# Seven-product matmul on one Trainium2 core: a new order of the products, T4 in its own bank, each operand sum in its own step, squares six steps ahead

## Chip, cores, metric

One core of a Trainium2 chip runs the whole program. The metric is device microseconds (us) of one execution, as a median of several. The kernel before takes 1394.89 us: three runs between 1392.15 and 1395.37.

## What is computed

```
attn = attention(q, k, v, phi)                    # linear attention over 32 memory slots, 8 x 8 heads, 576 tokens
x    = attn as 4608 tokens x 512
h    = x @ w_in1;   g  = max(h, 0)**2             # 512 -> 2048
x2   = g @ w_out1                                 # 2048 -> 512   "first out product"
h2   = x2 @ w_in2;  g2 = h2 * sigmoid(h2)         # 512 -> 2048
out  = g2 @ w_out2                                # 2048 -> 512   "second out product"
```

All in float32.

## The kernel before, in words

Five stretches follow each other in time: attention and `x @ w_in1` (to about 323 us of the span), the first out product (324 to about 683 us), `x2 @ w_in2` (683 to about 1042 us), the second out product (from about 1027 us to the end, its first steps interleaved with the last of the stretch before). The two out products are one function, `second()`, called with `square=True` for the first (its input is relu only, the square is still to be taken) and with `square=False` for the second.

**Seven products for eight.** `second()` cuts the tokens into 6 batches. In each batch input and weight are cut into 2 x 2 blocks, and four blocks of result C11, C12, C21, C22 come from seven block products instead of eight. The seven left operands are B11, B21, B22 and four sums: T1 = B12 - B11, T2 = B22 - T1, T3 = B22 - B12, T4 = B21 - T2. The right operands are combinations of the weight blocks, made in the background and held in six slots per weight tile (a seventh, product 6, is loaded into slot 1 when product 1 is done, by `next_w`). Product numbers are those of `PRODUCTS`: 0 B11, 1 B21, 2 T2, 3 T1, 4 T3, 5 B22, 6 T4, and before the change this is also the order in which they run.

**Steps.** Each product has four steps h; a step is 12 matmuls of 128x128 by 128x384 on TensorE (two weight tiles, two output halves, three each), so that a product has 48 matmuls and a batch 336. Float32 accuracy comes from splitting an operand into a high and a low part: the operand tile `c` of a step holds both. ScalarE casts the raw tile `r` to the high part (line L822), then VectorE subtracts to get the low part (L823). Of each group of three matmuls the second needs the low part. `AHEAD = 4`: in program order the operand of a step is made four steps before its matmuls. `c` tiles rotate through six buffers (`spool`), and these six are also those in which `x2 @ w_in2` keeps its results (`g2t`).

**Sums.** The raw tiles are 128x768. VectorE makes T1 at L810, T2 at L814, T3 at L816, T4 at L819, in place except T2, which has tiles of its own. In program order T1 and T2 are both made in the step of product T2, T3 in the step of T1, T4 in the step of T3. In the first out product ScalarE squares every raw tile in place (L796): in program order B11 and B21 in the steps of B11, B12 and B22 in the steps of B21.

**Accumulation.** The products gather in PSUM banks a, b, c (`psa`, `psb`, `psc`): B11, T2, T3, T4 in a, B21 in b, T1 and B22 in c. `evict` takes partial sums out between: u1 is a copy of a after B11, and C11 = u1 + b; u2 is a copy of a after T2, and C12 = u2 + c after B22; u3 is a copy of c after T1, and C22 = u3 + a after T3; C21 is a itself after T4, copied by ScalarE into `y` (L872) and stored by SyncE (L874). Copies are ScalarE's (L734, L739, L741), additions VectorE's (L732).

**What sets the order.** The text gives program order, waits and buffers; a scheduler, which plans with estimated times, then picks the final order of instructions on each engine. On an engine they run strictly in that order. In the background, during the first out product, ScalarE and VectorE also build the weights of the next stretch (L162 to L216).

Of the kernel before, what the change touches and what calls it, by code (L numbers as in the profile page):

```python
# [77 lines left out]
def attention_moe_moe(ctx: ExitStack, tc, q, kv, phi, w_in1, w_out1, w_in2, w_out2, out):  # L78
# [645 lines left out]

    PRODUCTS = (("B11", "a"), ("B21", "b"), ("T2", "a"), ("T1", "c"), ("T3", "a"), ("B22", "c"), ("T4", "a"))
    FIRST = (0, 1, 3)
    UTAG = {"u1": "u1", "u2": "u2", "u3": "u1"}

    def evict(n, t, s, c, copy3, done):


        add = lambda to, x, y: nc.vector.tensor_tensor(to, x, y, op=ALU.add)  # L732
        if n == 0:
            nc.scalar.copy(s("u1"), t["a"])  # L734
        elif n == 1:
            add(c("C11"), t["b"], s("u1"))
            done("C11", None)
        elif n == 2:
            nc.scalar.copy(s("u2"), t["a"])  # L739
        elif n == 3:  # L740
            copy3(s("u3"), t["c"])  # L741
        elif n == 4:
            add(c("C22"), t["a"], s("u3"))
            done("C22", None)
        elif n == 5:
            add(c("C12"), t["c"], s("u2"))
            done("C12", None)
        else:
            done("C21", t["a"])

    QS = 2
    NH = NQ // QS
# [10 lines left out]
    def second(src, order, square, to, weights, begin, tiles=tuple(range(10))):  # L763
# [27 lines left out]
                        if held:  # L791
                            held(dma)

        def squares(b, h, names):
            for name in names if square else ():
                ins = nc.scalar.activation(raw[b, name, h], raw[b, name, h], AF.Square)  # L796
                if b == 0 and name in SQUARED:
                    follow(ins, relus[SQUARED[name] + h])

        def combos(b, n, h):  # L800

            tt = nc.vector.tensor_tensor
# [32 lines left out]
        begin(quarters)  # L835
        for k in range(AHEAD):
            ahead(k)
        for k, (b, n, h) in enumerate(steps):
            ahead(k + AHEAD)
            bank = PRODUCTS[n][1]  # L840
            if h == 0 and n == 0:
                ps = [{} for _ in range(2)]
                st = [{} for _ in range(2)]
            if h == 0 and n in FIRST:
                for o in range(2):
                    ps[o][bank] = psum.tile([P, TH], F32, tag=bank, bufs=4 if bank == "a" else 2, name=f"ps{bank}")
            x = cc.pop((b, n, h))
            for u in range(QS):
                for o in range(2):
                    for m, (wi, xi) in enumerate(((0, 0), (0, 1), (1, 0))):  # L850
                        mm = nc.tensor.matmul(  # L851
                            ps[o][bank], W[h * QS + u][:, slot(n), wi, o * P:(o + 1) * P], x[:, xi, u],
                            start=(n in FIRST and h == u == m == 0), stop=(h == NH - 1 and u == QS - 1 and m == 2),
                            skip_group_check=True,
                        )
                        if u == o == m == 0:
                            begun.append(mm)
            next_w(weights, range(h * QS, h * QS + QS), n, b == TB - 1)
            if h < NH - 1:
                continue  # L860
            for o in range(2):
                def tile_s(u, o=o):
                    if u not in st[o]:
                        st[o][u] = upool.tile([P, TH], F32, tag=UTAG[u], name=u)
                    return st[o][u]

                def done(c, bank, o=o, b=b):
                    if bank is None:
                        y = tile_s(SUM[c], o)
                    else:  # L870
                        y = upool.tile([P, TH], F32, tag="u1", name="y")
                        nc.scalar.copy(y, bank)  # L872
                    oh, half = int(c[1]) - 1, int(c[2]) - 1
                    nc.sync.dma_start(to(b, 2 * oh + o, half), y)  # L874
                evict(n, ps[o], tile_s, lambda c: tile_s(SUM[c]), nc.scalar.copy, done)
# [7 lines left out]
    def begin_out1(quarters):  # L883
# [9 lines left out]
        for q in range(WR, WR + 2):  # L893
            for k in range(SLOTS):
                held(load_w(w1o, q, k))
        for k, name in enumerate(("B11", "B21", None)):
            for q in (*range(WR + 2, NQ), *range(WR)) if k == 1 else range(WR + 2, NQ):
                held(load_w(w1o, q, k))
            if name:
                quarters(0, (name,), held)  # L900
            if k == 1:
                quarters(0, ("B12", "B22"), held)
        for k in range(3, SLOTS):
            for q in range(WR + 2, NQ):
                held(load_w(w1o, q, k))

# [50 lines left out]
    for b in range(TB):  # L957
        for r in range(NQ // 2):
# [4 lines left out]
            for n, (_, bank) in enumerate(PRODUCTS):  # L963
# [12 lines left out]
                for q in qs:  # L976
                    def tile_s(u, q=q):
                        if u not in st[q]:
                            st[q][u] = upool.tile([P, TH], F32, tag=UTAG[u], name=u)
                        return st[q][u]  # L980

                    def done(c, src, q=q):
# [19 lines left out]

    def begin_out2(quarters):
        quarters(0, ("B11", "B21"))
        for q0, n0, n1 in ((0, 0, 4), (2, 0, 4), (4, 0, 2), (6, 0, 1), (6, 1, 2), (4, 2, 4), (6, 2, 3)):
# [5 lines left out]
        for n in range(3, SLOTS):  # L1011
            for q in (range(NQ) if n > 3 else (6, 7)):
                load_w(w2o, q, n)

    second(g2, tuple(c.replace("C", "B") for c in order2), False,
# [46 lines left out]
```

## Time and profile before

| what | value |
|---|---|
| median of 3 runs (lowest, highest) | 1394.89 us (1392.15, 1395.37) |
| the profiled execution: its own time | 1397.46 us |
| its span, first to last instruction | 1395.6 us |
| mean granted TensorE clock | 0.994 of full speed |
| TensorE (PE) busy | 1365.2 us, 98% of the span, 9349 matmuls |
| VectorE (DVE) busy | 967.8 us, 69% |
| ScalarE (ACT) busy | 791.9 us, 57% |
| DMA | 388 MB, mean 278 GB/s |

The profiled execution is 2.57 us above the median, and 1.86 us of it lie outside its span. PE is the engine that is nearly always busy; the other two have room on average, which says nothing yet about a single place.

### The profile page before, as it was taken

Reading aid. Unit: us, or ns where it says so; the run is one execution under the profiler, and the core shown is the slowest. Engines: PE = TensorE matmul, PEld = TensorE weight load, DVE = VectorE, ACT = ScalarE, POOL = GpSimd, SP = SyncE. Lnnn points to the kernel's source line nnn. Section 1 sums busy time; section 2 is a strip of 40 time slices with the busy share of each in tenths; the row PEclk is TensorE's granted clock in tenths of the full one; section 3 lists DMA queues with packets and bytes.
Section 4 is the critical chain, followed back from the end, with each engine's and each line's share of the span. In section 5 each row is a group of like instructions: output and inputs, shape, how many; then the busy total and the mean of one; then the engine's idle time right before and its main releaser. Section 6 shows DMA issues by size and latency. Waiting matters only on the chain.

```text
span 1395.6 us, 25373 instructions
## 1 busy us (share of the span) xinstructions
PE 1365.2 (98%) x9349; PEld 1317.2 (94%) x9349; DVE 967.8 (69%) x1578; ACT 791.9 (57%) x1305; POOL 21.8 (2%) x44
## 2 busy tenths in 40 slices
PE   7899999998999999999999999999998999999998
PEld 5778888898999999999999999999998999999998
DVE  4668777746698897979565756566447858768583
ACT  3656666667758768586355545555444444444442
POOL 0001000000000000000000000000000000000000
PEclk9999999999999999999999999999999999999999
DMA  9979999899888869789988787888998567564640
GB/s 318 367 235 335 351 351 323 299 340 338 268 276 286 285 229 337 259 291 319 354 298 298 257 305 269 281 290 281 365 398 311 160 227 235 190 230 155 227 155 35
DMA packets 208445, 388.25 MB, mean 278 GB/s; under 512 B 19264, under 2 KB 90944, under 8 KB 208320
## 3 DMA queue, kind: packets, MB, share of 16 engines
q1 hardware_dynamic: 208320, 386.62, 80.3%
q8 instruction: 74, 1.21, 0.3%
q14 instruction: 51, 0.42, 0.1%
HBM read 253.38 MB, written 133.17 MB: 277 GB/s over the span
## 4 chain that ended last, share of the span: by engine, by line
PE 83%; DMA 11%; DVE 3%; ACT 1%; issue 1%; SPq 0%; ACTq 0%; DVEq 0%
PE psa L851 28%; PE psc L851 14%; PE psa L970 14%; PE h L661 7%; PE psc L970 7%; PE psb L851 6%; PE psb L970 4%; DMA g<-gt 3%; DMA r<-g 2%; DMA kv<-kv 2%; DMA st<-moe_w_in 2%; PE pswp L463 1%; DMA a<-phi 1%; DMA ws<-w1o 1%; PE pskv L407 1%
## 5 line engine op out<-in xcount | busy, mean ns | idle before, releaser
L823 DVE TENSOR_TENSOR c<-r,c 128x768 fp32r<-128x768 f32 x336 | 316.2, 953 | 164.2 <-ACT c L822 162.4
L851 PE MATMUL psa<-c,ws 128*128 128x384 f32 x2304 | 416.5, 338 | 6.7 <-DVE c L823 4.4
L851 PEld LDWEIGHTS psa<-c,ws 128*128 128x128 f32 x2304 | 406.6, 190 | 8.2 <-DVE c L823 5.4
L822 ACT CAST c<-r 128x768 fp32r<-128x768 f32 x336 | 278.3, 835 | 221.4 <-PE psa L851 112.1
L970 PE MATMUL psa<-xc,ws 128*128 128x384 f32 x1152 | 217.3, 336 | 0.0
L661 PEld LDWEIGHTS h<-at,wp 128*128 128x128 f32 x1344 | 180.2, 188 | 31.0 <-ACT gt L671 18.2
L851 PE MATMUL psc<-c,ws 128*128 128x384 f32 x1152 | 205.7, 335 | 1.8 <-ACT c L822 1.8
L851 PEld LDWEIGHTS psc<-c,ws 128*128 128x128 f32 x1152 | 200.9, 188 | 2.2 <-ACT c L822 2.2
L970 PEld LDWEIGHTS psa<-xc,ws 128*128 128x128 f32 x1152 | 202.3, 188 | 0.0
L661 PE MATMUL h<-at,wp 128*128 128x288 f32 x1344 | 191.2, 299 | 6.4 <-ACT gt L671 6.4
L970 PE MATMUL psc<-xc,ws 128*128 128x384 f32 x576 | 110.9, 335 | 0.0
L851 PE MATMUL psb<-c,ws 128*128 128x384 f32 x576 | 105.3, 337 | 0.0
L851 PEld LDWEIGHTS psb<-c,ws 128*128 128x128 f32 x576 | 101.6, 189 | 0.0
L970 PEld LDWEIGHTS psc<-xc,ws 128*128 128x128 f32 x576 | 101.2, 188 | 0.0
L796 ACT ACTIVATE r<-r 128x768 f32<-128x768 f32 x96 | 79.4, 844 | 22.9 <-DMA r<-g 18.9
L671 ACT ACTIVATE gt<-h 128x576 f32<-128x576 f32 x112 | 72.2, 648 | 35.0 <-PE h L661 24.4
L205 DVE TENSOR_TENSOR pp<-pw,pp 128x256 f32<-128x256 f32 x148 | 62.9, 434 | 32.7 <-ACT pp L204 30.3
L204 ACT CAST pp<-pw 128x256 fp32r<-128x256 f32 x148 | 58.3, 405 | 39.4 <-PE psa L970 14.8
L984 ACT ACTIVATE g2t<-g2t 128x1152 f32<-128x1152 f32 x48 | 54.8, 1164 | 30.0 <-DVE g2t L732 26.8
L162 ACT CAST top<-st 128x256 f16<-128x256 bf16 (+1 forms) x112 | 58.1, 528 | 24.0 <-PE psa L970 12.0
L734 ACT COPY u<-psa 128x384 f32<-128x384 f32 x72 | 34.2, 476 | 57.0 <-DVE g2t L732 20.6
L166 DVE SCALAR_TENSOR_TENSOR pw<-st,top 128x256 int32<-128x256 int32 x96 | 40.3, 426 | 31.5 <-ACT top L162 31.0
(101 smaller groups left out, 1174.6 us busy)
## 6 DMA issues: line engine op xcount, KB each, us to landing
r<-g SPq DMA_DIRECT2D x192, 384.0 KB, 5.7
g<-g2t SPq DMA_DIRECT2D x48, 768.0 KB, 6.9
ws<-w2i SPq DMA_DIRECT2D x136, 256.0 KB, 5.2
ws<-w2o SPq DMA_DIRECT2D x136, 256.0 KB, 4.1
ws<-w1o SPq DMA_DIRECT2D x116, 256.0 KB, 4.3
g<-gt SPq DMA_DIRECT2D x64, 384.0 KB, 6.1
kv<-kv SPq DMA_DIRECT2D x32, 516.0 KB, 6.7
st<-moe_w_out SPq DMA_DIRECT2D x64, 256.0 KB, 5.6
```

Source lines behind the costliest of these rows:

```text
L162: ins = nc.scalar.copy(top.bitcast(F16).rearrange("p (n h) -> p n h", h=2)[:, :, 1], flat.bitcast(BF16).rearrange("p (n h) -> p n h", h=4) ...
L166: to_f32.last = nc.vector.scalar_tensor_tensor(f.bitcast(I32), flat.rearrange("p (n w) -> p n w", w=2)[:, :n, 1], 13, top, op0=ALU.logical ...
L204: held(nc.scalar.copy(hi, w[:, of]))
L205: tt(lo, w[:, of], hi.bitcast(F32), op=ALU.subtract)
L661: mm = nc.tensor.matmul(h[:, half, :HALF], wp[b, j][:, g, s, fo:fo + P], attnT[b][:, x, g, tk], start=(k == 0), stop=(k == len(ops) - 1),)
L671: relus.append(nc.scalar.activation(gt[:, f % 2].rearrange("p (h t) -> p h t", h=2), h[:, :, :HALF], AF.Relu))
L796: ins = nc.scalar.activation(raw[b, name, h], raw[b, name, h], AF.Square)
L822: nc.scalar.copy(c[:, 0], r(name))
L823: tt(c[:, 1], r(name), c[:, 0].bitcast(F32), op=ALU.subtract)
L851: mm = nc.tensor.matmul(ps[o][bank], W[h * QS + u][:, slot(n), wi, o * P:(o + 1) * P], x[:, xi, u], start=(n in FIRST and h == u == m == 0 ...
L970: mm = nc.tensor.matmul(ps[q][bank], W[q][:, slot(n), wi, k * P:(k + 1) * P], x[:, xi, k], start=(n in FIRST and k == 0 and m == 0), stop= ...
L984: nc.scalar.activation(gq[q][:, :3], gq[q][:, :3], AF.Silu)
```

## The change

The products run in the order B11, B21, T1, T2, B22, T3, T4 (`ORDER`); their numbers, operands and weights are the old ones, and the loads of the weights follow the new order. T4 is gathered in bank b, in a group of its own, instead of bank a: after T3 ScalarE copies bank a into u4, and C21 = u4 + b is a VectorE addition after T4; the copy into `y` is gone. Partial sums u1, u2, u4 share three buffers, u3 has two. Each sum is made in the step that uses it: T1 in T1's, T2 in T2's, T3 in T3's; T4 is made behind the low part of B22's step. Each square is issued on its own, two steps before its operand is made, so six steps before its matmuls, one per step over sixteen steps, and held behind the matmuls that have just been begun; the loads of a next batch's raw tiles move with them.

```diff
+    BANKS = {n: bank for n, (_, bank) in enumerate(PRODUCTS)} | {6: "b"}
+    ORDER = (0, 1, 3, 2, 5, 4, 6)
+    SQUARES = 2
+    OWN = {"u1": "u2", "u2": "u2", "u3": "u1", "u4": "u2"}
+    UBUFS = {"u1": 2, "u2": 3}
+    def evict_out(n, t, s, done):
...
+        elif n == 4:
+            nc.scalar.copy(s("u4"), t["a"])
+            add("u3", t["a"], s("u3"))
+            done("C22", "u3")
...
+        elif n == 6:
+            add("u4", t["b"], s("u4"))
+            done("C21", "u4")
...
-        def squares(b, h, names):
-            for name in names if square else ():
-                ins = nc.scalar.activation(raw[b, name, h], raw[b, name, h], AF.Square)
+        def squares(k):
+            b, n, h = steps[k]
+            i = ORDER.index(n)
+            if n == h == 0 and b:
+                quarters(b)
+            if square and i < 4:
+                name = ("B11", "B21", "B12", "B22")[i]
+                x = raw[b, name, h]
+                ins = nc.scalar.activation(x, x, AF.Square)
                 if b == 0 and name in SQUARED:
                     follow(ins, relus[SQUARED[name] + h])
+                else:
+                    hold(ins)
...
-            if n == 0:
-                squares(b, h, ("B11", "B21"))
-            elif n == 1:
-                squares(b, h, ("B12", "B22"))
-            elif name == "T2":
+            if name == "T1":
                 tt(r("B11"), r("B12"), r("B11"), op=ALU.subtract)
                 raw[b, "T1", h] = r("B11")
+            elif name == "T2":
                 if h == 0:
                     place_tiles(b, "T2")
                 tt(r("T2"), r("B22"), r("T1"), op=ALU.subtract)
-            elif name == "T1":
+            elif name == "T3":
                 tt(r("B12"), r("B22"), r("B12"), op=ALU.subtract)
                 raw[b, "T3", h] = r("B12")
-            elif name == "T3":
-                tt(r("B21"), r("B21"), r("T2"), op=ALU.subtract)
-                raw[b, "T4", h] = r("B21")
             c = cc[b, n, h] = spool.tile([P, 2, QS, TH], F32R, tag="g", name="c")
             nc.scalar.copy(c[:, 0], r(name))
             tt(c[:, 1], r(name), c[:, 0].bitcast(F32), op=ALU.subtract)
+            if name == "B22":
+                tt(r("B21"), r("B21"), r("T2"), op=ALU.subtract)
+                raw[b, "T4", h] = r("B21")
-        steps = [(b, n, h) for b in range(TB) for n in range(7) for h in range(NH)]
+        steps = [(b, n, h) for b in range(TB) for n in ORDER for h in range(NH)]
...
         def ahead(k):
             if k < len(steps):
-                b, n, h = steps[k]
-                if n == h == 0 and b:
-                    quarters(b)
-                combos(b, n, h)
+                combos(*steps[k])
+            if k + SQUARES < len(steps):
+                squares(k + SQUARES)
...
-            bank = PRODUCTS[n][1]
+            bank = BANKS[n]
...
-            if h == 0 and n in FIRST:
+            first = n in FIRST or n == 6
+            if h == 0 and first:
...
-        for k, name in enumerate(("B11", "B21", None)):
+        for k, name in ((0, "B11"), (1, "B21"), (3, None)):
...
-        for k in range(3, SLOTS):
+        for k in (2, 5, 4):
```

The lines have moved: the matmuls of `second()` are L851 before and L889 now; the low part L823 is L856; the sums T1, T2, T3, T4 are L810, L814, L816, L819 before and L845, L850, L852, L858 now; the additions L732 are L760. In the rows below the columns are line, operation, output tile, input tiles.

VectorE at the start of the first out product, batch 0, from behind B21's low parts to T2's first one. The raw tiles are B11 (then T1) in r_4427 and r_4428, B12 (then T3) in r_4445 and r_4446, B21 in r_4439, B22 in r_4451; T2 is in r_4560 before and in r_4635 now; two steps share a tile. Before:

```order
L810 TENSOR_TENSOR r_4427<-r_4445,r_4427 128x768 x2
L810 TENSOR_TENSOR r_4428<-r_4446,r_4428 128x768 x2
L814 TENSOR_TENSOR r_4560<-r_4451,r_4427 128x768
L816 TENSOR_TENSOR r_4445<-r_4451,r_4445 128x768
L819 TENSOR_TENSOR r_4439<-r_4439,r_4560 128x768
L814 TENSOR_TENSOR r_4560<-r_4451,r_4427 128x768
L816 TENSOR_TENSOR r_4445<-r_4451,r_4445 128x768
L823 TENSOR_TENSOR c_4563<-r_4560,c_4563 128x768
```

Now:

```order
L845 TENSOR_TENSOR r_4427<-r_4445,r_4427 128x768 x2
L856 TENSOR_TENSOR c_4554<-r_4427,c_4554 128x768
L856 TENSOR_TENSOR c_4575<-r_4427,c_4575 128x768
L845 TENSOR_TENSOR r_4428<-r_4446,r_4428 128x768 x2
L850 TENSOR_TENSOR r_4635<-r_4451,r_4427 128x768
L852 TENSOR_TENSOR r_4445<-r_4451,r_4445 128x768
L856 TENSOR_TENSOR c_4594<-r_4428,c_4594 128x768
L858 TENSOR_TENSOR r_4439<-r_4439,r_4635 128x768
L856 TENSOR_TENSOR c_4613<-r_4428,c_4613 128x768
L850 TENSOR_TENSOR r_4635<-r_4451,r_4427 128x768
L852 TENSOR_TENSOR r_4445<-r_4451,r_4445 128x768
L856 TENSOR_TENSOR c_4638<-r_4635,c_4638 128x768
```

The four low parts of T1 (c_4554 to c_4613) now stand between the sums; before, the first low part behind B21's was T2's, behind nine sums, and T1's came behind all of T2's.

VectorE at the same place of the second out product, batch 0 (c_11650 before and c_11674 now are B21's last operand, r_11670 and r_11771 T2's tiles). Before:

```order
L823 TENSOR_TENSOR c_11650<-r_11526,c_11650 128x768
L810 TENSOR_TENSOR r_11519<-r_11555,r_11519 128x768
L810 TENSOR_TENSOR r_11520<-r_11556,r_11520 128x768 x2
L814 TENSOR_TENSOR r_11670<-r_11561,r_11519 128x768
L816 TENSOR_TENSOR r_11555<-r_11561,r_11555 128x768
L819 TENSOR_TENSOR r_11525<-r_11525,r_11670 128x768
L814 TENSOR_TENSOR r_11670<-r_11561,r_11519 128x768
L816 TENSOR_TENSOR r_11555<-r_11561,r_11555 128x768
L823 TENSOR_TENSOR c_11673<-r_11670,c_11673 128x768
```

Now:

```order
L856 TENSOR_TENSOR c_11674<-r_11550,c_11674 128x768
L845 TENSOR_TENSOR r_11543<-r_11579,r_11543 128x768
L856 TENSOR_TENSOR c_11694<-r_11543,c_11694 128x768
L845 TENSOR_TENSOR r_11544<-r_11580,r_11544 128x768
L856 TENSOR_TENSOR c_11714<-r_11543,c_11714 128x768
L845 TENSOR_TENSOR r_11544<-r_11580,r_11544 128x768
L856 TENSOR_TENSOR c_11732<-r_11544,c_11732 128x768
L850 TENSOR_TENSOR r_11771<-r_11585,r_11543 128x768
L852 TENSOR_TENSOR r_11579<-r_11585,r_11579 128x768
L850 TENSOR_TENSOR r_11771<-r_11585,r_11543 128x768
L852 TENSOR_TENSOR r_11579<-r_11585,r_11579 128x768
L856 TENSOR_TENSOR c_11750<-r_11544,c_11750 128x768
```

Here too T1's low parts come first, one behind each sum of T1, and the sums of T2 and T3 stand behind three of them.

TensorE at the start of the first out product, batch 0, from the end of B21 (`ws_...` are the weight tiles). Before:

```order
L851 MATMUL psb<-c,ws_4406 128x384 x6
L851 MATMUL psa<-c,ws_428 128x384 x6
L851 MATMUL psa<-c,ws_429 128x384 x6
L851 MATMUL psa<-c,ws_430 128x384 x2
L851 MATMUL psc<-c,ws_428 128x384 x2
L851 MATMUL psa<-c,ws_430 128x384 x4
```

Now:

```order
L889 MATMUL psb<-c,ws_4406 128x384 x6
L889 MATMUL psc<-c,ws_428 128x384 x6
...
L889 MATMUL psc<-c,ws_4406 128x384 x6
L889 MATMUL psa<-c,ws_428 128x384 x6
L889 MATMUL psa<-c,ws_429 128x384 x6
L889 MATMUL psa<-c,ws_430 128x384 x2
L889 MATMUL psc<-c,ws_428 128x384 x2
L889 MATMUL psa<-c,ws_430 128x384 x4
```

The 48 matmuls of T1 into bank c now stand between B21 and T2.

## Rows read from the trace of the kernel before

**Rows 1.** Windows: length, PE, PEld, DVE, ACT, POOL busy (instructions); clock, DMA, GB/s.

```profile
343.00:365.00 22.00, 18.89 (x100) 18.25 (x99) 16.84 (x21) 14.75 (x21) 0.00 (x0) 0.92 0.72 239
365.00:1023.00 658.00, 658.00 (x3778) 658.00 (x3778) 462.38 (x754) 396.14 (x668) 0.00 (x0) 1.00 0.86 294
1042.50:1066.40 23.90, 20.32 (x99) 19.69 (x98) 23.90 (x29) 8.99 (x13) 0.00 (x0) 0.86 0.92 329
1066.40:1391.60 325.20, 325.20 (x1870) 325.20 (x1869) 225.50 (x266) 144.83 (x194) 0.00 (x0) 1.00 0.56 186
```

**Rows 2.** What PE waited for, 343 to 1392 us: total us, times, longest.

```profile
PE psa L851 <- DVE c L823: 4.1, 2, 2.8
PE psc L851 <- ACT c L822: 1.8, 1, 1.8
PE psa L851 <- ACT c L822: 0.8, 1, 0.8
```

**Rows 3.** Timeline of PE, first out product: start, duration, instruction, [idle before, releaser].

```profile
343.02 2.60 PE L851 MATMUL psa<-c,ws 128*128 128x384 f32 x14
347.47 0.62 PE L851 MATMUL psc<-c,ws 128*128 128x384 f32 x2 [1.84 <-ACT c L822]
349.35 7.62 PE L851 MATMUL psa<-c,ws 128*128 128x384 f32 x34 [1.26 <-DVE c L823]
```

**Rows 4.** Timeline of PE, second out product.

```profile
1042.58 6.08 PE L851 MATMUL psb<-c,ws 128*128 128x384 f32 x34
1049.45 0.61 PE L851 MATMUL psa<-c,ws 128*128 128x384 f32 x2 [0.79 <-ACT c L822]
1052.85 4.21 PE L851 MATMUL psa<-c,ws 128*128 128x384 f32 x12 [2.79 <-DVE c L823]
```

**Rows 5.** Window behind the second stop, columns as in Rows 1.

```profile
1054.00:1058.00 4.00, 4.00 (x14) 4.00 (x13) 4.00 (x6) 1.58 (x3) 0.00 (x0) 0.50 1.02 357
```

**Rows 6.** Timeline of DVE, first out product.

```profile
336.12 1.83 DVE L810 TENSOR_TENSOR r<-r 128x768 f32<-128x768 f32 x2 [1.86 <-ACT r L796]
337.87 0.95 DVE L814 TENSOR_TENSOR r<-r 128x768 f32<-128x768 f32 x1
...
347.89 0.55 DVE L732 TENSOR_TENSOR u<-psb,u 128x384 f32<-128x384 f32 x1
348.35 0.94 DVE L823 TENSOR_TENSOR c<-r,c 128x768 fp32r<-128x768 f32 x1
```

**Rows 7.** Timeline of ACT, first out product.

```profile
335.24 3.05 ACT L796 ACTIVATE r<-r 128x768 f32<-128x768 f32 x4
```

**Rows 8.** The page's costliest groups: busy us, mean ns; idle before, releaser.

```profile
L822 ACT CAST c<-r 128x768 fp32r<-128x768 f32 x336 | 278.3, 835 | 221.4 <-PE psa L851 112.1
```

**Rows 9.** Timeline of DVE, second out product.

```profile
1042.25 0.96 DVE L823 TENSOR_TENSOR c<-r,c 128x768 fp32r<-128x768 f32 x1 [1.12 <-DMA r<-g]
1043.12 0.95 DVE L810 TENSOR_TENSOR r<-r 128x768 f32<-128x768 f32 x1
...
1047.50 0.95 DVE L814 TENSOR_TENSOR r<-r 128x768 f32<-128x768 f32 x1
...
1051.85 0.95 DVE L823 TENSOR_TENSOR c<-r,c 128x768 fp32r<-128x768 f32 x1
```

**Rows 10.** Windows over batches 1 to 3 of the first out product.

```profile
386.00:420.00 34.00, 34.00 (x197) 34.00 (x196) 31.68 (x45) 19.86 (x33) 0.00 (x0) 1.00 0.83 279
420.00:560.00 140.00, 140.00 (x806) 140.00 (x805) 117.56 (x173) 107.10 (x172) 0.00 (x0) 1.00 0.83 282
```

**Rows 11.** Timeline of DVE in batch 1, T2's first low part.

```profile
405.17 1.82 DVE L823 TENSOR_TENSOR c<-r,c 128x768 fp32r<-128x768 f32 x2
```

**Rows 12.** Timeline of PE in batch 1, T2's matmuls.

```profile
407.32 8.17 PE L851 MATMUL psa<-c,ws 128*128 128x384 f32 x46
```

**Rows 13.** Timeline at the end: the last DVE addition and ACT's last copy.

```profile
1383.24 1.08 DVE L732 TENSOR_TENSOR u<-psc,u 128x384 f32<-128x384 f32 x2 [1.81 <-PE psc L851]
1391.60 1.00 ACT L872 COPY y<-psa 128x384 f32<-128x384 f32 x2 [11.16 <-PE psa L851]
```

More of the change, by code (lines that the diff above doesn't have):

```diff
@@ L749, in evict @@
             done("C21", t["a"])
+    ORDER = (0, 1, 3, 2, 5, 4, 6)
[3 more added lines that the diff above has]
+    def evict_out(n, t, s, done):
+        add = lambda to, x, y: nc.vector.tensor_tensor(s(to), x, y, op=ALU.add)
+        if n == 0:
+            nc.scalar.copy(s("u1"), t["a"])
+        elif n == 1:
+            add("u1", t["b"], s("u1"))
+            done("C11", "u1")
+        elif n == 2:
+            nc.scalar.copy(s("u2"), t["a"])
+        elif n == 3:
+            nc.scalar.copy(s("u3"), t["c"])
+        elif n == 4:
+            nc.scalar.copy(s("u4"), t["a"])
+            add("u3", t["a"], s("u3"))
+            done("C22", "u3")
+        elif n == 5:
+            add("u2", t["c"], s("u2"))
+            done("C12", "u2")
+        elif n == 6:
+            add("u4", t["b"], s("u4"))
+            done("C21", "u4")
     QS = 2
@@ L823, in combos @@
             tt(c[:, 1], r(name), c[:, 0].bitcast(F32), op=ALU.subtract)
-        steps = [(b, n, h) for b in range(TB) for n in range(7) for h in range(NH)]
+            if name == "B22":
+                tt(r("B21"), r("B21"), r("T2"), op=ALU.subtract)
+                raw[b, "T4", h] = r("B21")
+        steps = [(b, n, h) for b in range(TB) for n in ORDER for h in range(NH)]
         def ahead(k):
             if k < len(steps):
-                b, n, h = steps[k]
-                if n == h == 0 and b:
-                    quarters(b)
-                combos(b, n, h)
+                combos(*steps[k])
+            if k + SQUARES < len(steps):
+                squares(k + SQUARES)
         start = len(begun)
         begin(quarters)
+        for k in range(SQUARES):
+            squares(k)
         for k in range(AHEAD):
@@ L852, in second @@
                             ps[o][bank], W[h * QS + u][:, slot(n), wi, o * P:(o + 1) * P], x[:, xi, u],
-                            start=(n in FIRST and h == u == m == 0), stop=(h == NH - 1 and u == QS - 1 and m == 2),
+                            start=(first and h == u == m == 0), stop=(h == NH - 1 and u == QS - 1 and m == 2),
                             skip_group_check=True,
@@ L863, in tile_s, with done @@
                     if u not in st[o]:
-                        st[o][u] = upool.tile([P, TH], F32, tag=UTAG[u], name=u)
+                        st[o][u] = upool.tile([P, TH], F32, tag=OWN[u], bufs=UBUFS[OWN[u]], name=u)
                     return st[o][u]
[L867 to L872, printed above, removed]
+                def done(c, u, o=o, b=b):
                     oh, half = int(c[1]) - 1, int(c[2]) - 1
-                    nc.sync.dma_start(to(b, 2 * oh + o, half), y)
-                evict(n, ps[o], tile_s, lambda c: tile_s(SUM[c]), nc.scalar.copy, done)
+                    nc.sync.dma_start(to(b, 2 * oh + o, half), tile_s(u, o))
+                evict_out(n, ps[o], tile_s, done)
         return [tiles[2 * places[-1][name] + k] for name in FREED for k in range(2)]
@@ L978, in tile_s @@
                         if u not in st[q]:
-                            st[q][u] = upool.tile([P, TH], F32, tag=UTAG[u], name=u)
+                            st[q][u] = upool.tile([P, TH], F32, tag=UTAG[u], bufs=UBUFS[UTAG[u]], name=u)
                         return st[q][u]
@@ L1004, in begin_out2 @@
         quarters(0, ("B11", "B21"))
-        for q0, n0, n1 in ((0, 0, 4), (2, 0, 4), (4, 0, 2), (6, 0, 1), (6, 1, 2), (4, 2, 4), (6, 2, 3)):
+        for q0, n0, n1 in ((0, 0, 4), (2, 0, 4), (4, 0, 2), (6, 0, 1), (6, 1, 2), (4, 2, 4), (6, 3, 4)):
             for n in range(n0, n1):
@@ L1010, in begin_out2 @@
                 quarters(0, ("B12", "B22"))
-        for n in range(3, SLOTS):
-            for q in (range(NQ) if n > 3 else (6, 7)):
+        for n in (2, 5, 4):
+            for q in (range(NQ) if n > 2 else (6, 7)):
                 load_w(w2o, q, n)
```

## The prediction

> **What bounds the kernel now.** I first asked whether TensorE ever stops in the two out products, since the whole-span share, 98% busy, can't say where. The list of its waits from 343 us to the end has only four stops, 6.7 us together, all for an operand `c` [rows 2]. The timelines put them at two places: the first out product at 346 to 349 us, where T2's matmuls and two of T1's wait 1.84 and 1.26 us [rows 3], and the second at 1048.6 to 1053 us, where T2's first step waits 0.79 us for ScalarE's cast and 2.79 us for VectorE's low part [rows 4]. Between these places nothing is left to win: 3778 matmuls fill 658.00 us, 174.2 ns each, and 1870 fill 325.20 us, 173.9 ns each [rows 1].
>
> What the two places cost is more than the idle time. I count matmuls: 22.00 us held 100 of them, which take 17.4 us at 174 ns, so **4.6 us** are lost; 23.90 us held 99, which take 17.2 us, so **6.7 us** [rows 1]. Idle alone is 3.1 and 3.6 us. The rest is the clock: behind the idle, twelve matmuls took 4.21 us, twice their time [rows 4], and from 1054 to 1058 us the engine is busy all 4.00 us with 14 matmuls at a granted clock of 0.50, the 1.2 GHz level [rows 5]; over the first place's 22 us it was 0.92 [rows 1]. So a microsecond of idle cost 4.6/3.1 = 1.5 at the first place and 6.7/3.58 = 1.9 at the second.
>
> Here a page weighs in. The Trainium skill, "Perfetto Trace Analysis", section "Identifying the Most-Contended Engine", holds that busy time of matmuls tells little of the distance to the limit, and names the work done or the busy share of weight loads instead. By weight loads the loss would be (22.00 - 18.25) + (23.90 - 19.69) = 8.0 us and the forecast about 1388. The trace agrees on busy time, but weight loads too fill all 4.00 us of the throttled window [rows 5], so the count decides.
>
> Why it waits there: after B21 the kernel runs T2, whose operand needs two sums, and both are queued together. In the first out product VectorE runs L810, L814, L816 and L819 one behind the other from 336.12 us, and T2's second low part starts only at 348.35 us [rows 6]. In the second, T2's first low part starts at 1051.85 us, nine instructions behind B21's last [rows 9]. VectorE is full there, 23.90 of 23.90 us [rows 1], and its last wait for a transfer ends at 1042.25 us [rows 9].
>
> **The change, part by part.** Matmuls, weights, operand splits and squares keep their number; the 192 sums only change their place; 24 copies into `y` become 24 copies into u4 and 24 additions.
>
> *Order and sums.* T1 needs one sum, so PE has T1's 48 matmuls (8.36 us at 174 ns) before it asks for T2. I walked VectorE's new order at the spacing of the old one: 0.87 us for a sum or low part (two in 1.75 us, 336.12 to 337.87), 0.46 for an addition (347.89 to 348.35) [rows 6]. First place: T1's second pair of sums needs squares of B12. ScalarE's squares begin at 335.24 us, four in 3.05 [rows 7]; now one cast stands ahead (0.835 [rows 8]) and one square must end (0.8): 336.9. From there to T2's second low part stand sixteen long instructions and two additions, 336.9 + 16 x 0.87 + 2 x 0.46 = 351.8 us. PE begins T2 at 343.02 + 8.36 = 351.4 and asks for that low part sixteen matmuls later, at 354.2. Spare: 2.4 us. T1's own low parts end at 336 to 343 us, ahead of their use. So I take **-4.6 us**.
>
> Second place: PE ends what it can do of B21 at 1042.58 + 34 x 0.174 = 1048.5 us [rows 4]. T1's first sum starts at 1043.12 as now [rows 9], its cast and low part end at about 1046.7, the next two at 1048.5 and 1050.4, asked for at 1048.7, 1050.8 and 1052.9. Then it gets tight. Of the six operand buffers two still hold results of the stretch before and one the last operand of B21, whose last weights come late, so three rotate. T1's fourth low part stands behind four sums of T2 and T3: 1050.4 + 5 x 0.87 = 1054.8 against 1055.5; T2's four come by my walk at 1056.5, 1060.0, 1063.5 and 1065.3 against 1057.2, 1060.3, 1063.8 and 1065.9. The spare, 0.3 to 0.7 us, is no larger than the walk's error. I take **-6.7 us** and give back half a microsecond of idle at 1.9, **+1.0**. Bounds: 0, and 6.7 if all of it stays.
>
> The Trainium skill, "TensorE: Matmul & The Clock Gate", section "What's actually happening", says that the throttled state is the default and activity releases it. By it a short stop between busy stretches would cost only its own 0.5 us, and the sum would be 0.5 us lower. The rows show the price of long stops only.
>
> *T4 in bank b.* Within a batch this is off PE's path: u4's copies and C22's additions have the 8.36 us of T4. At the very end C21 is now an addition pair instead of a copy pair: 1.08 us for the pair against 1.00 [rows 13], **+0.1**. Twenty-two further additions of 0.46 us lie on VectorE beside PE's work. Where the first out product gives way to the next stretch, bank b must be emptied by those additions before it is used again: my walk has them done at about 683.7 us against a need at 686.7, so 0, with up to 2 us (a little over one pair) as the other end.
>
> *Squares and raw loads.* One square per step instead of clumps of four [rows 7]; ScalarE is busy 107.10 of 140.00 us in these batches [rows 10] and has room. The loads of raw tiles on SyncE's queue are issued two steps (4.2 us) earlier in the program. Nothing in either lies on PE's path, which has no wait between 365 and 1023 us. Cost 0; if cover fails it shows as the second rival below. A gain is excluded, as PE has no idle there.
>
> *Sum*, on the profiled execution's own 1397.46 us: -4.6 - 6.7 + 1.0 + 0.1 = 1387.3. That execution is 2.57 us above the median, so against 1394.89 the forecast is **1384.7 us**.
>
> **Rivals.** (1) *Only the first place is won.* The second has no spare, and VectorE is saturated there: each instruction more than I counted, or a late raw tile, puts the wait at T1's fourth or T2's second step. If the whole 6.7 us stay: 1394.89 - 4.6 + 0.1 = 1390.4; if half: 1387. For it: three rotating buffers, DMA share 1.02 [rows 5]. Against: PE gets 8.36 us more before T2.
>
> (2) *VectorE late in batches 1 to 5 of the first out product: slower.* It is busy 31.68 of 34.00 us in batch 1 and 117.56 of 140.00 later [rows 10], and T2's first low part ends at 406.1 us [rows 11] while its matmuls begin at 407.32 [rows 12]: 1.2 us ahead. In the new order the sums of T2, T3 and T4 stand close together behind T1, with the weights' work and the new additions. Counting VectorE's work against 2.09 us a step, it falls back by 5.8 to 6.1 us in each batch, where the old order fell back by 2.6 to 5.1. With six buffers a low part can be five steps early less cast and subtraction, 5 x 2.09 - 1.8 = 8.65 us, and ScalarE's own queue takes some 1 to 1.5 of it: I get a spare of 1 to 1.5 us in each batch. If it were missing and x us idle came in each of five batches, the loss would be 5 x 1.9 x = 9.5 x: half a microsecond gives 1389.5; from x = 1.1 the gain is eaten; from x = 1.5 the kernel is slower by over 0.3%; at 1.8, 1402. For it: the share of 93% in batch 1. Against: no such wait today, and a spare of the right sign in my count.
>
> (3) *The change only moves the wait.* In the new order too T2's and T3's sums stand in pairs for both steps of a tile. If T2's second step were still late by as much, the time would be within 2 us of 1394.9. The walk speaks against it, as T1's matmuls cover 8.36 us, more than the 3.1 and 3.6 us of idle.
>
> (4) *Border or T4.* A wait on bank b or on u4's buffers: 1 to 3 us, so 1386 to 1388; nothing in the rows shows such a wait now.
>
> **How the numbers follow.** A measurement of this kernel can tell about 0.3%, 4.2 us, from no change: 1390.7 to 1399.1 counts as the same. Both places won, 1382 to 1387.5: 0.57. One place partly left, small lateness or a border wait, 1387.5 to 1390.7 (rivals 1 and 4, mild 2): 0.21. Gain eaten (3, or 2 with x about 1): 0.15. Slower (2 with x over 1.5): 0.07. So faster 0.78, same 0.15, slower 0.07. The lower end can't lie far below 1394.89 - 11.3 + 0.1 = 1383.7, and the runs shown reach 2.7 us below their median: 1381.5. The upper end takes in rival 1 whole with 1 us more: 1391.5.
>
> **What would show it.** Right: no stop of PE between 343 and 352 us, about 126 matmuls in a window of 22 us there, clock 1.00; at most half a microsecond of stops where bank c follows bank b in the second out product; PE at 174 ns a matmul through batches 1 to 5; the last addition about 1.1 us long. Wrong: waits of PE for L856 in every batch (rival 2), waits at T1's fourth step or T2's with the clock at 0.50 behind them (rival 1), or a wait for L760 at 683 us (rival 4). A gain above 14 us would mean that I missed a place before 343 us, where the orders are alike.

## The result and the profile after

The changed kernel takes 1380.47 us (median of four runs, 1379.26 to 1381.61) beside 1394.1 us for the kernel before (four runs): a ratio of 0.9909, interval 0.9895 to 0.9924. A second comparison with more runs gave 1381.33 us beside 1392.57 us (6 and 23 runs): 0.9919, interval 0.9901 to 0.9936. So it is faster by 11 to 14 us, where 10.2 us were forecast, and the first median lies 1.0 us below the forecast's range of 1381.5 to 1391.5 us.

The profiled execution of the changed kernel took 1379.26 us, with a span of 1377.4 us and a mean granted clock of 1.000. What PE waited for from 319 us to the end, against [rows 2]:

```profile
PE psa L889 <- ACT c L855: 1.5, 1, 1.5
PE psa L889 <- DVE c L856: 0.4, 1, 0.4
```

Both waits are for the very first operand of the first out product, its cast and then its low part, with two matmuls between; below they are called the stop at the first operand. The kernel before has it too, with the same length, but in its trace the matmuls behind it were slower. PE's timeline there, first the kernel before, then now:

```profile
324.00 0.62 PE L851 MATMUL psa<-c,ws 128*128 128x384 f32 x2 [1.46 <-ACT c L822]
324.99 9.84 PE L851 MATMUL psa<-c,ws 128*128 128x384 f32 x46 [0.37 <-DVE c L823]
```

```profile
319.00 0.62 PE L889 MATMUL psa<-c,ws 128*128 128x384 f32 x2 [1.46 <-ACT c L855]
320.00 8.28 PE L889 MATMUL psa<-c,ws 128*128 128x384 f32 x46 [0.37 <-DVE c L856]
```

The stops of [rows 3] and [rows 4] are gone. The same two stretches by matmuls, with the columns of [rows 1], each begun where the product behind B21 begins or, in the second, where PE's last piece of B21 begins, and the rest of the second out product:

```profile
336.47:358.47 22.00, 22.00 (x128) 22.00 (x128) 19.71 (x26) 12.72 (x19) 0.00 (x0) 1.00 0.81 268
1031.02:1054.92 23.90, 23.90 (x139) 23.90 (x139) 23.64 (x28) 12.52 (x18) 0.00 (x0) 1.00 0.92 340
1054.92:1373.80 318.88, 318.88 (x1830) 318.57 (x1829) 229.98 (x278) 142.23 (x192) 0.00 (x0) 1.00 0.57 188
```

128 matmuls instead of 100 in 22 us, 139 instead of 99 in 23.9 us, at the full clock: nothing is lost at either place. PE's timeline at the two places (start, duration, instruction, count):

```profile
328.11 8.52 PE L889 MATMUL psb<-c,ws 128*128 128x384 f32 x48
336.47 8.52 PE L889 MATMUL psc<-c,ws 128*128 128x384 f32 x48
344.83 2.62 PE L889 MATMUL psa<-c,ws 128*128 128x384 f32 x14
...
1031.02 6.08 PE L889 MATMUL psb<-c,ws 128*128 128x384 f32 x34
1036.94 6.79 PE L889 MATMUL psc<-c,ws 128*128 128x384 f32 x38
1043.56 0.52 PE L889 MATMUL psa<-c,ws 128*128 128x384 f32 x2
1043.92 1.90 PE L889 MATMUL psc<-c,ws 128*128 128x384 f32 x10
1045.66 2.26 PE L889 MATMUL psa<-c,ws 128*128 128x384 f32 x12
1047.75 1.23 PE L889 MATMUL psb<-c,ws 128*128 128x384 f32 x6
1048.82 2.25 PE L889 MATMUL psa<-c,ws 128*128 128x384 f32 x12
```

T1's 48 matmuls in bank c now stand between B21 and T2, and no row has an idle time in front of it. How close it is in the second product stands in VectorE's timeline, against [rows 9]: the low parts (L856) of T1's fourth and of T2's first three steps.

```profile
1042.40 0.95 DVE L856 TENSOR_TENSOR c<-r,c 128x768 fp32r<-128x768 f32 x1
...
1044.14 0.95 DVE L856 TENSOR_TENSOR c<-r,c 128x768 fp32r<-128x768 f32 x1
...
1047.61 0.95 DVE L856 TENSOR_TENSOR c<-r,c 128x768 fp32r<-128x768 f32 x1
...
1051.09 0.95 DVE L856 TENSOR_TENSOR c<-r,c 128x768 fp32r<-128x768 f32 x1
```

They end at 1043.35, 1045.09, 1048.56 and 1052.04 us. PE takes up the matmuls that need the first three at 1043.92, 1045.66 and 1048.82 us: 0.6, 0.6 and 0.3 us later. At the end C21 is an addition, against [rows 13]:

```profile
1373.33 1.08 DVE L760 TENSOR_TENSOR u<-psb,u 128x384 f32<-128x384 f32 x2 [6.77 <-PE psb L889]
```

It lasts as long as the addition pair of [rows 13], 0.08 us longer than the copies that it replaces.

### The profile page after: what moved, and what is told of

Same layout as the page of the kernel before. It is cut to its first block, busy times and chain, and to the rows that moved or that the text cites. A ratio compares the mean times of both kernels' runs of the same rounds, so it can differ in the third digit from the quotient of the medians.

```text
span 1377.4 us, 25465 instructions
## 1 busy us (share of the span) xinstructions
PE 1356.8 (99%) x9349; PEld 1311.7 (95%) x9349; DVE 982.6 (71%) x1602; ACT 796.1 (58%) x1305; POOL 21.5 (2%) x44
## 4 chain that ended last, share of the span: by engine, by line
PE 88%; DMA 9%; SPq 1%; ACT 1%; DVE 1%; issue 0%; ACTq 0%; DVEq 0%
PE psa L889 22%; PE psb L889 15%; PE psa L1003 15%; PE psc L889 15%; PE h L661 9%; PE psc L1003 7%; PE psb L1003 4%; DMA st<-moe_w_in 2%; DMA a<-phi 2%; DMA g<-gt 1%; DMA w1o<-pp 1%; PE pswp L463 1%; PE pskv L407 1%; DMA q<-q 1%; DMA r<-g 1%; DMA kv<-kv 1%
## 5 line engine op out<-in xcount | busy, mean ns | idle before, releaser
L856 DVE TENSOR_TENSOR c<-r,c 128x768 fp32r<-128x768 f32 x336 | 316.5, 955 | 141.4 <-ACT c L855 140.5
L889 PE MATMUL psa<-c,ws 128*128 128x384 f32 x1728 | 310.7, 336 | 1.8 <-ACT c L855 1.5
L889 PEld LDWEIGHTS psa<-c,ws 128*128 128x128 f32 x1728 | 301.8, 188 | 2.4 <-ACT c L855 1.7
L889 PE MATMUL psc<-c,ws 128*128 128x384 f32 x1152 | 207.9, 335 | 0.0
L889 PE MATMUL psb<-c,ws 128*128 128x384 f32 x1152 | 206.3, 336 | 0.0
L889 PEld LDWEIGHTS psc<-c,ws 128*128 128x128 f32 x1152 | 201.3, 188 | 0.0
L889 PEld LDWEIGHTS psb<-c,ws 128*128 128x128 f32 x1152 | 201.2, 188 | 0.0
L1003 PE MATMUL psb<-xc,ws 128*128 128x384 f32 x288 | 56.9, 336 | 0.0
```

Of the source, the lines that this page charges most:

```text
L889: mm = nc.tensor.matmul(ps[o][bank], W[h * QS + u][:, slot(n), wi, o * P:(o + 1) * P], x[:, xi, u], start=(first and h == u == m == 0), st ...
L1003: mm = nc.tensor.matmul(ps[q][bank], W[q][:, slot(n), wi, k * P:(k + 1) * P], x[:, xi, k], start=(n in FIRST and k == 0 and m == 0), stop= ...
```

## The experiments

**Both kernels again, and each out product alone.** The first two are the kernels as they are. The other two keep both versions of `second()` in one program and call the new one for one out product; the loads of the old one's weights go back to their old order with it (cut here):

```diff
-    second(g2, ...)          # out1_new: the second out product stays old
+    second_old(g2, ...)
...
-    free = second(g1, ...)   # out2_new: the first out product stays old
+    free = second_old(g1, ...)
```

> The changed kernel as it is, timed again and traced again. Theory A, the two stops are the whole gain: 4.6 and 6.7 us less, 0.1 us more at the end, so a ratio near 0.992 (1382.9 us against 1394.1), and what the first comparison showed beyond it is scatter between executions; the start of the first out product then lies anywhere between 318 and 325 us in a trace of either kernel. Theory B, a third place gains 2 to 3 us as well (the stretch ahead of the first out product, which was 5.0 us shorter in the first trace, or the clock in its first product): a ratio near 0.990, and the first out product starts at about 319 us again.

> The kernel before, timed and traced once more. Both theories: a ratio of 1 within 0.2%, PE stops of 3.1 us at 343 to 350 us and 3.6 us at the start of the second out product, and 4.6 and 6.7 us lost there by the count of matmuls. Theory A: the first out product starts earlier or later than 324.0 us by some us, and its first 46 matmuls take 8.0 or 9.8 us by chance. Theory B: it starts at 324 us and its first 46 matmuls take 9.8 us again.

> The first out product as changed, the second as before. Theory A: -4.6 us, ratio 0.9967, PE without a stop in the first out product and with 3.6 us of stops at the start of the second, 6.7 us lost there by count. Theory B: the third place goes with the first out product, where loads of weights are issued in a new order: -7 us, ratio 0.995.

> The second out product as changed, the first as before. Both theories: -6.6 us, ratio 0.9953; PE stops 3.1 us at the start of the first out product and nowhere in the second. If the two places hung together, this and the run with only the first changed would not add up to the whole.

Measured, ratio to the kernel before: 0.9919 (0.9901 to 0.9936) for the change, 1.0002 (0.9989 to 1.0014) for no change, 0.9967 (0.9954 to 0.9979) with the first product new and 0.9967 (0.9951 to 0.9982) with the second new. By these ratios that is -11.3, -4.6 and -4.6 us; the medians alone would give -11.2, -4.2 and -2.6. The parts add to 9.2 us, and with their intervals that is the whole. The 6.6 us forecast for the second place are inside its interval, at the edge. The 5.0 us by which the first out product began earlier in the changed kernel's first trace (319.00 us against 324.00) are scatter: in the fourteen traces of this document it begins between 317.7 and 324.2 us, in a second trace of the changed kernel at 320.93, in a second one of the kernel before at 321.24, with the first product alone new at 324.17. So theory A holds so far; theory B's 0.990 lies just outside the interval. Its other candidate, the slow first product, came again as theory B had it, with 9.82 us in before_again and 8.27 in after_again; the last section takes it up.

The new trace of the kernel before shows why a single profiled execution sizes this badly. Its second place, in a window as long as that of [rows 1]'s third row, and PE's timeline there:

```profile
1039.84:1063.74 23.90, 20.33 (x108) 19.69 (x108) 23.90 (x29) 10.13 (x15) 0.00 (x0) 0.93 1.02 372
```

```profile
1046.71 0.62 PE L851 MATMUL psa<-c,ws 128*128 128x384 f32 x2 [0.79 <-ACT c L822]
1050.11 3.64 PE L851 MATMUL psa<-c,ws 128*128 128x384 f32 x12 [2.79 <-DVE c L823]
1053.59 1.20 PE L851 MATMUL psb<-c,ws 128*128 128x384 f32 x6
```

The idle times are those of [rows 4] to the hundredth, 0.79 and 2.79 us, but the twelve matmuls behind them took 3.64 us instead of 4.21, and the next six 1.20 instead of 2.12. That is 108 matmuls instead of 99, and a loss of 5.1 us instead of 6.7. With the first out product alone changed it was 5.3 us. At this place the idle time belongs to the kernel; what the clock adds behind it belongs to the execution.

**The order alone, and everything but the order.**

```diff
 # order_only: new order, each sum in its own step; T4 in bank a, squares in the old clumps (cut)
-    BANKS = {...} | {6: "b"}
+    BANKS = {...}
         elif n == 6:
-            add("u4", t["b"], s("u4"))
+            nc.scalar.copy(s("u4"), t["a"])
 # bank_squares: old order, sums (cut) and weight loads (cut); T4 in bank b, squares ahead
-    ORDER = (0, 1, 3, 2, 5, 4, 6)
+    ORDER = (0, 1, 2, 3, 4, 5, 6)
```

In bank_squares B12 and B22 are still squared in pairs, since T2, third in the old order, needs both; only B11's and B21's squares stand on their own.

> The new order with each sum in its own step, but T4 gathered in bank a as before (C21 copied out of a by ScalarE) and the squares and raw loads where they were. Theory A: order and place of the sums are the whole gain at the two places, and bank b and the squares are worth nothing there: no stop of PE at the two places, ratio near 0.992. Rival: T4 now follows T3 in the same bank, so its first matmul must wait until the addition for C22 has read bank a, half a microsecond and more after T3's end in each of twelve batches: waits of PE for L760 of 7 to 12 us in all, ratio 0.997 to 1.000, unless the scheduler puts other matmuls between.

> The old order with the sums where they were, but T4 in bank b with u4 and C21 added up by VectorE, and the squares on their own six steps ahead. Theory A: no gain, ratio 1.000 within 0.2%, and the stops of PE at both places stay (3.1 and 3.6 us of idle). Rival: squares in single steps free VectorE's first sums earlier and bring part of the 4.6 us: 0.998. It also shows whether the first 46 matmuls of the first out product take 9.8 us (all three traces with the old order of that product) or 8.3 us (all three with the new).

Order alone: 1391.03 us, ratio 0.9991 (0.9971 to 1.0011). The gain is gone, and my theory A with it, though not by the rival that I had put up: PE waits for no addition. Its waits from 325 us to the end:

```profile
PE psa L882 <- ACT c L849: 5.3, 3, 2.4
PE psa L882 <- DVE c L850: 1.4, 3, 0.5
```

The two places themselves are free of stops. The new stops all lie where T4 begins, in batches 0, 1, 2 and 4 of the first out product, for instance in batch 0, where ScalarE works without a gap on casts (L849) and on squares of the next batch (L825), one of which had waited for its load:

```profile
359.69 0.85 ACT L825 ACTIVATE r<-r 128x768 f32<-128x768 f32 x1 [2.32 <-DMA r<-g]
...
374.19 0.82 ACT L849 CAST c<-r 128x768 fp32r<-128x768 f32 x1
```

```profile
364.76 8.52 PE L882 MATMUL psa<-c,ws 128*128 128x384 f32 x48
375.06 9.19 PE L882 MATMUL psa<-c,ws 128*128 128x384 f32 x42 [1.77 <-ACT c L849]
```

Everything but the order: 1401.45 us, ratio 1.0071 (1.0046 to 1.0095), so 8 us slower by the medians and 10 by the ratio. The stops at both places stay, and five new ones come, one in each of batches 1 to 5, this one in batch 1:

```profile
406.94 1.01 DVE L760 TENSOR_TENSOR u<-psb,u 128x384 f32<-128x384 f32 x2
407.87 0.94 DVE L857 TENSOR_TENSOR c<-r,c 128x768 fp32r<-128x768 f32 x1
```

```profile
407.42 0.52 PE L887 MATMUL psc<-c,ws 128*128 128x384 f32 x2
408.87 4.43 PE L887 MATMUL psa<-c,ws 128*128 128x384 f32 x22 [0.93 <-DVE c L857]
```

In the old order VectorE has T2's, T3's and T4's sums and C11's pair of additions ahead of that low part, and is 0.93 to 1.09 us late in each batch, 5.0 us in all. This is what rival 2 of the prediction feared, but in the old order. Which of the two parts brings it, bank b with its additions or the squares, no run separates.

**The order with one of the other two.** Each run gives order_only one of its two missing parts back.

```diff
 # order_bank: order_only, and
+    BANKS = {...} | {6: "b"}
 # order_squares: the changed kernel, and
-    BANKS = {...} | {6: "b"}
+    BANKS = {...}
```

> The new order, each sum in its own step, and T4 in bank b with u4; squares and raw loads stay in the old clumps, four steps ahead. Theory C, the late squares are what ate the gain of the order-only run (ScalarE queued casts of T3, T4 and the next B11 behind squares that waited for their loads): stops of PE for ScalarE's casts at the end of batches, some 5 to 7 us, stay; ratio 0.997 to 0.999. Theory D, the shared bank a ate it (T3 and T4 interleaved by halves, casts wait for buffers that PE frees late): no stops in batches 1 to 5, ratio 0.992.

> The new order, each sum in its own step, and the squares and raw loads six steps ahead; T4 stays in bank a, C21 is copied out of it. Theory C: no stop of PE for casts, at most short waits for the additions that read bank a between T3 and T4; ratio 0.992 to 0.994. Theory D: stops at the end of batches as in the order-only run, ratio 0.997 to 0.999.

Measured: 0.9913 (0.9893 to 0.9934) with bank b, 0.9919 (0.9896 to 0.9942) with the early squares. Neither trace has a stop of PE between the first operand and the end, but for 0.17 us in the second. So theories C and D were both too simple: either part removes all the stops of order_only, and only the lack of both brings them. With bank b ScalarE is just as full before T4 in batch 0, 8.40 of 8.40 us in the window over T3, with the columns of [rows 1], first of order_only, then of order_bank, and behind them order_bank's PE, without a stop:

```profile
364.76:373.16 8.40, 8.40 (x49) 8.21 (x48) 5.53 (x8) 8.40 (x14) 0.00 (x0) 1.00 1.01 344
```

```profile
363.99:372.39 8.40, 8.40 (x50) 8.40 (x50) 5.94 (x10) 8.40 (x14) 0.00 (x0) 1.00 0.93 338
```

```profile
363.99 8.52 PE L883 MATMUL psa<-c,ws 128*128 128x384 f32 x48
372.35 8.52 PE L883 MATMUL psb<-c,ws 128*128 128x384 f32 x48
```

In this batch much of the difference is not the bank's. Counted from PE's first matmul of the first out product, the square that waits for its load starts at the same time, 37.45 us behind it in order_only and 37.33 in order_bank. But in order_bank's trace the first product was slow (9.83 us for 46 matmuls), and T3 begins 44.1 us behind the first matmul instead of 42.5: PE came 1.6 us later, nearly the whole of the 1.77 us stop. Why bank b leaves no stop in batches 1, 2 and 4 either, the runs do not tell.

**How much room VectorE has in batches 1 to 5.** The sum for T2 is made twice, with the same result, in its first two steps (dose_half) or in all four (dose1).

```diff
-                tt(r("T2"), r("B22"), r("T1"), op=ALU.subtract)
+                for _ in range(2 if square and b and h < 2 else 1):   # dose1: without h < 2
+                    tt(r("T2"), r("B22"), r("T1"), op=ALU.subtract)
```

> The changed kernel, and in batches 1 to 5 of the first out product the sum for T2 is made twice in its first two steps: 1.74 us more on VectorE ahead of T2's second low part. By the trace of the changed kernel that low part is some 2.2 us early: no stop, ratio as the changed kernel, 0.992. By the prediction's count (spare 1 to 1.5 us): 0.3 to 0.7 us of stop in each of five batches, 1380 us + 3 to 7.

> The same in all four steps of T2, 3.5 us more per batch; the scheduler also puts some of it ahead of T2's second low part. By the trace's spare of 2.2 us: one stop of about 1.1 us in each of five batches, 5.5 us of idle, so 1387 us if a stop costs itself and 1389 to 1392 us if it costs 1.5 to 1.9 times itself through the clock. By the prediction's spare: 2 to 2.5 us a batch, 1392 to 1405 us.

Measured: 1390.12 us, 0.9975 (0.9961 to 0.9989), and 1392.18 us, 0.9998 (0.9985 to 1.001). The smaller dose already stops PE in each of the five batches, by 0.2 to 1.3 us (0.52, 1.02, 0.21, 0.63 and 1.28): so 1.74 us more of VectorE's time are 0.2 to 1.3 us too much, and by this dose the room is 0.5 to 1.5 us, about as the prediction counted (1 to 1.5 us). The larger dose, 3.48 us a batch, stops PE by only 0.8 to 1.9 us a batch (1.22, 1.86, 0.77, 1.36 and 1.63), which would leave a room of 1.6 to 2.7 us, as I had read it from the trace (2.2 us). Neither reading can take the order as fixed: ahead of T2's second low part in batch 5 the smaller dose has four of T4's sums, the larger only two. So the room is 0.5 to 2.7 us, by the order that the scheduler picks, and the two doses do not settle it further. The larger dose, in PE's waits:

```profile
PE psa L890 <- DVE c L857: 4.1, 6, 1.6
PE psc L890 <- ACT c L856: 2.7, 2, 1.4
```

These two traces also price short stops. With the clock at 1.00 throughout, from 365 to 680 us, the smaller dose first:

```profile
365.00:680.00 315.00, 311.32 (x1773) 307.88 (x1772) 277.98 (x402) 224.81 (x355) 0.00 (x0) 1.00 0.83 283
```

```profile
365.00:680.00 315.00, 307.95 (x1752) 304.25 (x1751) 284.82 (x410) 224.38 (x352) 0.00 (x0) 1.00 0.82 278
```

315 us hold 1809 matmuls at 174.1 ns. The smaller dose misses 36, 6.3 us, for 3.66 us of idle in eight stops; the larger misses 57, 9.9 us, for 6.84 us in eight. In these two executions a short stop costs its idle time and 0.3 to 0.4 us, without any fall of the clock. But the two are among the fastest of their kernels, 1386.76 and 1388.32 us. The medians are 8.8 and 10.9 us above the changed kernel's 1381.33, so per microsecond of the traces' idle time the stops cost 2.4 and 1.6 us there. With the smaller dose the four shortest executions, 1386.3 to 1387.3 us, have a mean granted clock of 0.999 or 1.000, the six others, 1390.1 to 1392.3 us, one of 0.997 to 0.999; with the larger, three at 1.000 took 1388.3 to 1390.6 us, seven at 0.996 to 0.998 took 1390.8 to 1395.6. So longer times go with a lower clock; whether it fell behind these stops, no trace shows.

**The stop that is left.** In early_cast the cast of the first operand stands ahead of ScalarE's last relu.

```diff
+            ins = nc.scalar.copy(c[:, 0], r(name))
+            if square and b == n == 0 and h < 1:
+                follow(relus[-1], ins)
```

> The changed kernel, and the cast of the very first operand of the first out product stands ahead of ScalarE's last relu of the stretch before, in an idle gap of 0.9 us that the trace of the changed kernel shows at 316.7 to 317.6 us. PE's stop of 1.46 us for that cast should go, the wait for its low part stay at 0.4 us or grow to 1: 1.0 to 1.4 us less than the changed kernel, ratio 0.991.

> The kernel before once more, for its trace alone. If the fall of the clock in the first product of the first out product belongs to this kernel, its first 46 matmuls take 9.8 us for the fourth time; if it is chance, 8.3 us may come. The stops of 3.1 and 3.6 us at the two places are the same in any case, while what the clock adds there may differ by 1.5 us from trace to trace.

Measured: 1379.53 us, 0.9892 (0.9874 to 0.9909), the fastest of all; against the change alone the intervals overlap, so the time does not prove it, but the trace shows one stop of 0.74 us in place of 1.46 and 0.37:

```profile
320.02 8.61 PE L891 MATMUL psa<-c,ws 128*128 128x384 f32 x48 [0.74 <-ACT gt L671]
```

before_look, one execution of the kernel before at 1394.82 us, showed the slow first product again, 9.81 us for 46 matmuls: by the expectation above, a sign that it belongs to this kernel and is not chance. Its loss at the second place was 100 matmuls in 23.9 us, 6.5 us.

## Why the prediction was right or wrong

**The mechanism was right at the two places.** The stops were where the counts said, T1's 8.36 us of matmuls cover T2's two sums, and both stops went whole. The walk of VectorE's order held to 0.2 us. Counted from the end of PE's last piece of B21, it had T1's fourth and T2's first three low parts at 6.3, 8.0, 11.5 and 15.0 us; measured from 1036.94 us they end at 6.4, 8.2, 11.6 and 15.1 us. The price at the end, 1.08 us for the pair, was right as well.

**The step that failed is a term of the sum**: the +1.0 us given back for half a microsecond of idle in the second product. It was no reading but a margin for the walk's error, put into the middle of the forecast instead of its range, and it measured 0: no stop there. Without it the forecast ratio is 0.9920, and the larger comparison gave 0.9919. That they agree so closely is luck: the 6.7 us of the second place were those of one trace, four traces have 5.9 on average, and with 5.9 the ratio would be 0.9925. Against the first median the forecast of 1384.7 us was 4.2 us too high; the other 3.2 us are these.

The base is the largest. I subtracted from a median of three runs, 1394.89; with 23, 24 and 7 runs the kernel before is at 1392.57, 1393.03 and 1392.81, some 2.3 us lower. (Beside the first comparison's own four runs, 1394.1 us, the base is 0.8 us off and 2.4 us are left.) The lower end of the range was also miscalculated: the prediction's 1383.7 less its 2.7 is 1381.0, not 1381.5, and neither allows anything for so few runs.

What is left, 1 to 2.4 us, is inside the interval of the first comparison. A part of it may be the slow first product, 9.84 us against 8.28, which the prediction didn't count and which neither of the two traces of the changed kernel has; the runs leave that open (see the last section).

**The price per microsecond of idle**, 1.5 and 1.9, was taken as a property of the stop. The second place lost 6.7, 5.1, 6.5 and 5.3 us in four traces with the same 3.58 us idle, and stops up to 1.6 us cost 0.3 to 0.4 us beyond themselves with the clock at 1.00, but more at the medians of the dose runs. By an estimate from the two dose traces half a microsecond would have cost 0.8 to 0.9 us in such an execution, by chance close to my 1.0. The Trainium skill, "TensorE: Matmul & The Clock Gate", section "What's actually happening", has activity release the throttle, from which I took it that a short stop costs only itself. The two dose traces agree as to the clock, and differ by those 0.3 to 0.4 us; six traces with a fall behind 1.46 and 0.37 us of idle do not agree.

**T4's bank and the squares: "cost 0, a gain is excluded"** was wrong in its reason, and so was the whole -4.6 and -6.7 us under "Order and sums": those alone brought 2.0 us (1391.03 against 1393.03). PE had no idle in those batches in the old order, but in the new one it would have: without both, 5.3 and 1.4 us of stops eat the gain. Either of them is worth 10 to 11 us in the new order and, beside the other, nothing that these runs can tell. In the old order the two together cost 8 to 10 us. The rows of the kernel before could not show this, and I judged the parts one at a time. The sum did not suffer, since the change held both parts; as far as the prediction goes, that is luck.

**The rivals.** Rival 1 did not come: 0.3 us of room at the tightest step was enough. Rival 2 did not come in the changed kernel; its room of 1 to 1.5 us lies within the 0.5 to 2.7 us of the two doses, and in the old order, with bank b and the early squares, it decides. Rival 3 is out. Rival 4 did not show: PE did not wait for L760 anywhere in the changed kernel's traces.

## What to carry to other kernels

When an engine stops because its next operand needs two dependent sums, put a piece of work that needs only one of them in between, and count the matmuls in the window, not the busy share, to see what it is worth. Judge the parts of a change in the order that they will run in: a reserve that costs nothing where nothing waits can be what holds the gain once another order uses up the slack. Keep margins for a walk's error in the range, and take the base from as many runs as there are.

## What the runs showed of the hardware

The clock's answer to stops of one and the same length differs from trace to trace. The stop of 1.46 and 0.37 us at the first operand has the same length, within 0.02 us, in thirteen traces of ten kernels (early_cast has another). In six of them the next 46 matmuls took 9.77 to 9.84 us, in seven 8.26 to 8.28. In the first trace of the kernel before, the windows of the next microseconds, columns as in [rows 1], and behind them one window of the changed kernel's trace at the same distance from its stop, read

```profile
325.00:326.00 1.00, 1.00 (x4) 1.00 (x5) 1.00 (x2) 1.00 (x2) 0.00 (x0) 0.59 1.08 401
326.00:327.00 1.00, 1.00 (x5) 1.00 (x4) 1.00 (x2) 1.00 (x3) 0.00 (x0) 0.50 1.15 394
327.00:328.00 1.00, 1.00 (x5) 1.00 (x4) 1.00 (x2) 0.60 (x1) 0.00 (x0) 0.50 1.00 360
```

```profile
321.00:322.00 1.00, 1.00 (x7) 1.00 (x7) 1.00 (x2) 1.00 (x3) 0.00 (x0) 1.00 1.31 381
```

The granted clock falls to 0.50, the 1.2 GHz level, one to two microseconds after PE has begun to work again at 324.00 us, with the engine busy from 324.99 us on. In the changed kernel's trace the same microseconds show 1.00. So this stop costs either itself or 1.6 us more, 0.1% of the time.

What decides it is open. At the second place one kernel shows both a longer and a shorter fall behind the same idle time (99, 108 and 100 matmuls in 23.9 us in the three traces of the kernel before), so there it is the execution. At the first operand no kernel shows both answers. All four traces in which batch 0 of the first out product is the old one have the fall (three of the kernel before, one of out2_new); none of the five in which it is the changed one has it (two of the changed kernel, out1_new and the two doses); of the four other kernels, with a trace each, order_bank and order_squares have it. So it may go with the kernel rather than with chance, and then some 1.6 us of the gain belong to it, a third place that no experiment here isolates. Against that stands that the mean granted clock differs between executions of one kernel: 0.996 to 1.000 in the changed kernel's ten, and up to 0.999 in out2_new, whose trace has three falls and 0.996. But where the clock fell in those, no trace shows.
